# Attention key-value tails as full-row matmuls over zero-padded values, with a new instruction order

## The chip, the cores and the metric

The kernel runs on one core of a Trainium2 chip. The time is device microseconds of one execution of the whole kernel; the median of a few executions counts, and less is better. A profile is one further execution, recorded instruction by instruction.

## What is computed

Linear attention with cosine weights over 8 batches, 8 heads, 576 positions and a head dimension of 64, followed by a two-layer network with a squared ReLU on the 4608 x 512 result (weights 512 x 2048 and 2048 x 512):

```python
def phi(x, c, s):
    r = np.maximum(x, 0.0)
    return np.concatenate([r * c, r * s], axis=-1)
q_p = phi(q, cos_w, sin_w)
k_p = phi(k, cos_w, sin_w)
kv = np.einsum('bhsf,bhsd->bhfd', k_p, v)
z = np.sum(k_p, axis=2)
num = np.einsum('bhsf,bhfd->bhsd', q_p, kv)
den = np.einsum('bhsf,bhf->bhs', q_p, z)[..., None] + 1e-06
attn = num / den
...
h = x @ w_in
r = np.maximum(h, 0.0)
g = r * r
y = g @ w_out
```

## The kernel before

**Attention.** The 576 positions of a batch are four tiles of 128 positions (j = 0 to 3) and a tail of 64 (j = 4, in the code `J`). The tails of an even and an odd batch share tiles: the even batch's 64 positions lie in partitions 0 to 63, the odd batch's in 64 to 127 (`rows(b)`). Raw tails are loaded into `kt`, `vt` and `qt`, one load for each batch. The features of key tails go to `kpt`; from batch 2 on, one instruction with all 128 partitions makes them for both batches of a pair. The values are cast to bf16 by `att_v` into `vext` (four tiles, two buffers, by `b % 2`) and into `vextt` (the tail; two buffers, by `b // 2 % 2`, each holding a pair of batches). Column 64 of each head in these tiles is one, so that one product gives the sums and the normalizer together.

`att_kv` (matmuls at L400) multiplies key features by values: 8 heads x 4 tiles of 128x65 with 128 partitions contracted, then 8 tail matmuls with the batch's own 64 partitions. `att_kvz` copies the result to SBUF, `att_num` (L526) multiplies by query features, and `att_div` divides. Batch 0 has a path of its own (`first_ones`, `first_kv`; L414 and L431). Query features are transposed on TensorE for batches 0 and 1 (`att_qT_pe`, L499), by DMA later.

**The two layers.** The work is done per batch of 512 positions (m = 0 to 7), with the tails of all batches as a ninth block (m = 8). From block 2 on each product is made from seven half-size products instead of eight: L698 for the first layer, L887 for the second, both 128x256 matmuls. Between products with a shared accumulator ScalarE copies PSUM banks (`seed`: L1108 and L1190; others at L1125, L1200 and L1213) and applies the ReLU (L714); VectorE adds (L721, L1196), squares (L631), and forms sums of operands (L656, L680, L847, L866). Earlier blocks use plain products (L615, L748, L774, L788). L382 are filler matmuls on zeros, at the start and in the first stage.

**The order.** The program first records every step as an operation of a plan (`add`: engines, duration, reads, writes), and each reading or writing of a named resource orders it behind others. `ORDER` is a written-out list of all operations with an engine for each (`p` TensorE, `a` ScalarE, `v` VectorE, `g` GpSimd, `s` the DMA queue of SyncE). `Plan.run` records them in exactly this order, so each engine's queue, the SyncE queue included, has the order of the list. Many features, casts and squares can go to either ScalarE or VectorE; the list says which. `plan_v` and `plan_kv` add the operations for values and the key-value product. The loads of the main tiles are at L218, of tails at L257, DMA transposes at L490 and L558, stores at L813.

Of the kernel before, what the change touches and what calls it, by code (L numbers as in the profile page):

```python
# [15 lines left out]
FP = 512  # L16
# [9 lines left out]
117v 128a 122p 138a 145v 129p 143a 306v 140a 124p 83g 123a 146p 130a 84g 148p 125a 147v 131p 126a
149v 133p 85g 171v 168v 150p 166v 134a 142v 167a 151p 169v 132a 172v 152p 174v 170a 173v 135a 153p
86g 154p 87g 155p 156p 177v 88g 176a 178v 175a 181p 179v 180v 182p 183p 157p 250s 184a 89g 332v 185p
158p 253s 186v 159p 257s 258s 191p 189p 254s 187p 192v 160p 251s 190v 252s 195p 188v 161p 196v 255s
193p 162p 194a 334v 199p 197p 249s 163p 200v 164p 198v 256s 285v 201p 278v 165p 202a 286v 279a 209p  # L30
207v 210p 203a 218p 280v 211a 261v 206a 259v 215p 260v 281a 216p 264v 212p 219a 262v 282s 221p 217a
263v 284v 283a 227p 271v 266a 272v 287s 269v 225p 270a 268v 265a 273v 213p 267v 222a 274p 307v 421s
226a 275p 214a 276p 230p 309v 277a 420s 228a 234p 204v 231a 288p 223p 235a 299s 289v 244p 298s 224a
419s 290p 229a 232p 291v 236p 220v 292s 233a 293p 239p 245a 294v 237a 418s 241p 240a 416s 439v 238a
295p 441v 246p 445v 296v 310p 247a 311p 440v 438a 297s 301v 242a 312p 444v 308v 300a 417s 313p 243a
302s 248v 314p 443a 333v 344p 424a 446v 315p 427v 423a 447s 428v 422a 316p 340v 429v 425a 341v 345p
342v 360p 431v 346a 361p 426v 317p 347a 432v 442s 430v 362a 343v 348p 433v 363a 349p 350a 303p 364p
205s 351a 304v 365p 366a 573s 353p 352p 367a 355v 434p 354v 368p 458s 369p 358v 574s 356p 370v 435p
459s 371v 357a 436p 208s 372p 374v 437a 397p 572s 335v 373a 381p 569s 319v 398a 448p 396p 318a 571s
449v 380p 399a 321p 570s 382a 359v 400p 383a 568s 401p 402a 450p 384p 403a 451v 322p 386a 597a 405p  # L40
601v 452s 453p 599a 385p 407v 404p 454v 387a 323p 566s 594a 406v 388p 305s 375a 389p 390v 324p 391v
565s 392p 460a 410v 408p 376v 393a 455p 325p 394v 409a 456v 411a 326p 378v 457s 327p 395v 596a 328p
567s 577v 493p 329a 330v 509p 580a 412v 466p 461a 595v 468p 602v 600a 462s 575v 584a 469p 578v 603s
414v 585a 467p 489v 470a 576v 581v 510p 598s 471a 490v 494p 377v 511a 474p 495a 583v 491v 512a 475p
379v 589a 320s 337v 513p 496a 717s 514p 492v 515a 463p 413v 497p 516a 464v 498p 718s 586a 517p 331s
499a 518p 579v 472p 519v 500a 588a 415v 501p 587a 590p 582a 503v 713s 521p 520v 502p 714s 522a 591p
336v 716s 592p 523v 546p 504v 593a 505p 547a 339v 545p 506a 604p 338v 530p 548a 529p 605v 531a 473p
476a 507v 532a 606p 735v 549p 477a 607v 533p 551a 550p 535a 534p 737v 608s 552a 609p 741v 478p 736v
536a 610v 738a 715s 537p 524a 553p 539v 554p 538p 555v 611p 556v 480p 729a 612v 508a 557p 479p 540v
613s 742v 541p 558a 482v 481p 542a 739s 559v 743a 485p 543v 740v 544a 560v 486p 744s 657p 637v 641p  # L50
727v 487a 730v 642p 721a 638v 488s 658p 483v 643a 614p 640v 659a 484s 720v 615p 644a 871s 561v 660a
639v 868s 645p 724a 525v 661p 870s 725a 646p 723v 869s 722v 662p 663a 562v 616p 647a 864s 728v 664a
527v 617p 865s 648a 526v 719a 666p 563v 618a 649p 726a 665p 651v 650p 863s 619a 731p 668v 862s 653p
667v 732p 652v 654a 755s 733p 669p 671v 734a 756s 655v 677p 528v 670a 694p 867s 745p 693p 695a 746v
678p 696a 622p 679a 656v 747p 680a 697p 897a 620p 748v 894a 681p 891v 892a 749s 698p 672v 699a 750p
682p 700a 623p 866s 896v 683a 751v 465s 702p 684a 701p 898a 673v 685p 893a 686p 687v 621p 624a 703v
882a 752p 564v 689p 625a 705p 886a 753v 626p 899a 704v 706a 754s 628p 758a 884v 707v 627p 690a 688v
895s 877a 629p 691v 630v 692a 790p 875v 900s 633p 757v 631v 634p 872a 786v 708v 759s 791p 635a 807p
792a 787v 806p 709v 763p 793a 789v 885a 883v 794p 808a 788v 1010s 795p 675v 796a 764p 1011s 809a
881v 710v 880a 632s 765p 876v 797a 810p 878v 874a 879v 798p 812a 873v 799p 800v 811p 1013s 760p 711v  # L60
1012s 813a 802p 761v 766p 1014s 1015s 814p 801v 767a 887p 636s 816v 803a 888p 1053s 768a 804v 889p
1027v 1052s 815p 712v 890a 771p 805a 817v 826p 674v 762s 901p 843p 1025v 820v 827p 1026a 902v 818p
844a 769p 819a 676v 828a 772p 821v 829a 903p 770p 773a 904v 830p 774a 842p 1024v 905s 832a 1016v
906p 831p 822v 845a 775p 1021v 833a 1018v 1017a 846p 907v 847p 848a 776p 1019v 849a 1022v 908p 1032a
835p 909v 851p 1037a 834p 1033a 850p 853v 910s 1034a 777p 779v 1038a 852v 778p 1020a 836v 782p 1054a
780v 1023a 854p 837v 1035a 838p 934v 1028p 855a 856v 1036s 935v 955p 839a 823v 939p 956a 936v 938p
857v 940a 954p 1029p 941a 1030p 825v 957a 783p 1031a 840v 937v 1040a 958p 841v 942p 784a 1042p 960a
959p 1039v 944a 943p 858v 1041s 1055a 911p 1043v 945a 912p 961a 859v 785s 963p 860v 781s 947p 861v
946p 1056s 962p 965v 913p 948v 914p 949v 964v 950p 915a 1044p 968v 966p 951a 952v 975p 824v 916a
974p 967a 1045v 991p 976a 919p 953v 977a 1046s 990p 992a 1047p 917p 993a 1048v 969a 978p 994p 995p  # L70
979p 996a 970v 1049p 920p 997a 972v 980a 998p 1050v 921a 918p 981a 1000v 1051s 999p 922a 971v 982p
983p 984v 925p 985v 986p 1001v 1002p 987a 988v 923p 1004v 1003a 1083v 924p 1005a 1084v 1085v 1088p
927v 1104p 1087p 1086v 1089a 989v 930p 1090a 1105a 1057p 1006v 1091p 1092p 1007v 1093a 1103p 931p
1008v 1094a 1106a 1058v 926p 932a 1095p 1059s 928v 1107p 1108p 1097v 1109a 1096p 933s 1009v 1062p
1110a 929s 1098v 1112p 973v 1111p 1101v 1099p 1114v 1063p 1100a 1113v 1124p 1117v 1064a 1140p 1125a
1123p 1182v 1115p 1126a 1060p 1116a 1141a 1127p 1118v 1128p 1129a 1139p 1061p 1130a 1142a 1132p
1065a 1143p 1134v 1144p 1145a 1131p 1183v 1068p 1146a 1184v 1102a 1133v 1147p 1148p 1137v 1187p
1149v 1135p 1119v 1188a 1069p 1136a 1150v 1151p 1070a 1153v 1203p 1138v 1152a 1066p 1204a 1202p
1121v 1067p 1185v 1205a 1154v 1186p 1071a 1207p 1189a 1120v 1206p 1072p 1155v 1208a 1073p 1157v
1209a 1156v 1190p 1076v 1191p 1192a 1211p 1079p 1193a 1213v 1074p 1195p 1194p 1197v 1080p 1210p  # L80
1081a 1196v 1075p 1082s 1200v 1198p 1212v 1239p 1158v 1199a 1223p 1240a 1216v 1214p 1077v 1222p
1215a 1159p 1122v 1078s 1224a 1217v 1238p 1225a 1161p 1241a 1201v 1227p 1226p 1243p 1228a 1162p
1229a 1242p 1218v 1163a 1160p 1244a 1220v 1231p 1246a 1245v 1230p 1164a 1233v 1247p 1248p 1232v
1165p 1249v 1236v 1234p 1250v 1251p 1235a 1167p 1252v 1254a 1237v 1168p 1255v 1166p 1253v 1169a
1260p 1170a 1219v 1261p 1256v 1257v 1171p 1262a 1258v 1172p 1173p 1175v 1174p 1263p 1176v 1178p
1259v 1177s 1221v 1179p 1264p 1180a 1268p 1181s 1265a 1269p 1266g 1267g 1271p 1270a 1272p 1274p
1273a 1275p 1281p 1276a 1277a 1282p 1278v 1286p 1280g 1283v 1279g 1290p 1285s 1287a 1289g 1284s
1291a 1288g 1293a 1292s
"""


class Plan:

# [49 lines left out]
def kernel(  # L143
# [9 lines left out]
    nc = tc.nc  # L153
    P = nc.NUM_PARTITIONS
    B, H, S, D = q.shape
# [1363 lines left out]
```

## Time and profile before

| | us |
|---|---|
| runs | 272.72, 273.38, 273.41 |
| median | 273.38 |
| profiled execution, its own time | 272.29 |
| span in its profile | 270.5 |
| TensorE busy | 264.0 (98%) |
| VectorE busy | 217.1 (80%) |
| ScalarE busy | 199.3 (74%) |

PE is TensorE's matmul side and PEld its weight loads, DVE is VectorE, ACT ScalarE, POOL GpSimd, SP SyncE with its DMA queue. `L400` is line 400 of the kernel. A row of the timeline has the start, the length in us, engine, line, operation, output and inputs, the shapes, and the count of merged instructions; in square brackets stand the idle time of the engine before and what ended it. The chain is the work that ended last, followed back from the end. A matmul's record includes its way through the array, so the records of a dense stream overlap, and its pace is read from starts or from the chain's pieces.

### The profile page before, as it was taken

Reading aid. Unit: us, or ns where it says so; the run is one execution under the profiler, and the core shown is the slowest. Engines: PE = TensorE matmul, PEld = TensorE weight load, DVE = VectorE, ACT = ScalarE, POOL = GpSimd, SP = SyncE. Lnnn points to the kernel's source line nnn. Section 1 sums busy time; section 2 is a strip of 40 time slices with the busy share of each in tenths; the row PEclk is TensorE's granted clock in tenths of the full one; section 3 lists DMA queues with packets and bytes.
Section 4 is the critical chain, followed back from the end, with each engine's and each line's share of the span. In section 5 each row is a group of like instructions: output and inputs, shape, how many; then the busy total and the mean of one; then the engine's idle time right before and its main releaser. Section 6 shows DMA issues by size and latency. Waiting matters only on the chain.

```text
span 270.5 us, 6697 instructions
## 1 busy us (share of the span) xinstructions
PE 264.0 (98%) x2710; PEld 212.8 (79%) x2710; DVE 217.1 (80%) x455; ACT 199.3 (74%) x330; POOL 18.6 (7%) x33
## 2 busy tenths in 40 slices
PE   8999999999999999999999999999999999999993
PEld 3787555655587688998999889899988888888882
DVE  1774866898978999999999999999799679779401
ACT  3885971699969989899899978994966696373131
POOL 8345000000000000000000000000000000000013
PEclk9999999999999999999999999999999999999999
DMA  7999999799999999989999999639311300210134
GB/s 210 256 206 287 321 258 358 199 247 261 285 288 307 250 228 254 384 169 235 284 277 199 213 348 314 83 80 271 41 40 41 139 0 0 80 78 4 78 119 116
DMA packets 86142, 52.79 MB, mean 195 GB/s; under 512 B 56960, under 2 KB 82944, under 8 KB 86112
## 3 DMA queue, kind: packets, MB, share of 16 engines
q1 hardware_dynamic: 78624, 42.87, 61.3%
q0 software_dynamic: 7136, 9.37, 16.0%
q8 instruction: 21, 0.34, 0.5%
q10 hardware_dynamic: 352, 0.13, 0.2%
q14 instruction: 9, 0.07, 0.1%
HBM read 36.70 MB, written 9.44 MB: 171 GB/s over the span
## 4 chain that ended last, share of the span: by engine, by line
PE 90%; DMA 6%; DVE 0%; SPq 0%; ACT 0%; issue 0%; POOL 0%; POOLq 0%; DVEq 0%
PE bank L698 32%; PE bank L887 31%; DMA q<-in_q_dram 6%; PE bank L615 6%; PE bank L774 5%; PE bank L788 5%; PE abank L400 3%; PE abank L526 3%; PE bank L499 1%; PE bank L599 1%; PE bank L431 1%; PE abank L382 0%; DVE qp L358 0%; PE bank L563 0%; SPq L245 0%
## 5 line engine op out<-in xcount | busy, mean ns | idle before, releaser
L698 PE MATMUL bank<-xT,w1sb 128*128 128x256 bf16 x336 | 47.7, 273 | 0.0
L698 PEld LDWEIGHTS <-w1sb 128*128 128x128 bf16 x448 | 42.7, 98 | 6.3
L887 PEld LDWEIGHTS <-gT 128*128 128x128 bf16 x448 | 43.6, 98 | 5.1
L714 ACT ACTIVATE gT<-bank 128x512 bf16<-128x512 f32 x56 | 32.6, 598 | 15.2 <-PE bank L698 14.9
L887 PE MATMUL bank<-w2sb,gT 128*128 128x256 bf16 x336 | 41.9, 273 | 0.0
L721 DVE TENSOR_TENSOR gT<-bank,qpTp 128x512 bf16<-128x512 f32 x56 | 36.7, 685 | 5.7 <-PE bank L698 5.3
L887 PEld LDWEIGHTS <-gs 128*128 128x128 bf16 x336 | 32.7, 98 | 3.7
L698 PEld LDWEIGHTS <-w1t 128*128 128x128 bf16 x336 | 32.2, 98 | 4.1
L1108 ACT COPY bank<-bank 128x512 f32<-128x512 f32 x56 | 31.8, 581 | 3.1 <-PE bank L698 1.8
L698 PE MATMUL bank<-qpTp,w1t 128*128 128x256 bf16 x224 | 31.5, 273 | 0.0
L887 PE MATMUL bank<-w2t,gs 128*128 128x256 bf16 x224 | 28.0, 273 | 0.0
L629 ACT ACTIVATE gT<-gT 128x2048 bf16<-128x2048 bf16 (+1 forms) x15 | 27.8, 1855 | 0.3
L631 DVE TENSOR_TENSOR gT<-gT 128x2048 bf16<-128x2048 bf16 (+1 forms) x19 | 22.5, 1191 | 1.3 <-ACT gT L714 1.2
L541 DVE TENSOR_TENSOR x<-abank,rden 128x512 bf16<-128x512 f32 x30 | 20.7, 692 | 1.0
L615 PE MATMUL bank<-xT,w1sb 128*128 128x512 bf16 x84 | 19.9, 379 | 0.0
L821 POOL DMA_DIRECT2D out_dram<-ysb x4 | 2.4, 614 | 235.3 <-ACT ysb L1200 230.5
L1196 DVE TENSOR_TENSOR ysb<-bank,y 128x512 f32<-128x512 f32 x14 | 9.6, 688 | 10.7 <-ACT bank L1249 7.6
L1125 ACT COPY qpTp<-bank 128x512 f32<-128x512 f32 x28 | 16.2, 590 | 0.6 <-PE bank L698 0.6
L698 PE MATMUL bank<-xT,w1t 128*128 128x256 bf16 x112 | 16.3, 273 | 0.0
L698 PE MATMUL bank<-zeros,w1sb 128*128 128x256 bf16 x112 | 16.0, 273 | 0.0
L1200 ACT COPY ysb<-bank 128x512 f32<-128x512 f32 x13 | 7.6, 587 | 10.6 <-PE bank L887 10.5
L774 PE MATMUL bank<-w2sb,gT 128*128 128x512 bf16 x64 | 15.1, 379 | 0.0
(128 smaller groups left out, 432.8 us busy)
## 6 DMA issues: line engine op xcount, KB each, us to landing
out_dram<-ysb SPq DMA_DIRECT2D x16, 512.0 KB, 4.1
q<-in_q_dram SPq DMA_DIRECT2D x13, 512.0 KB, 6.9
v<-in_v_dram SPq DMA_DIRECT2D x12, 512.0 KB, 5.4
k<-in_k_dram SPq DMA_DIRECT2D x12, 512.0 KB, 6.5
w1sb<-in_moe_w_in_dram POOLq DMA_DIRECT2D x4, 512.0 KB, 9.7
w2sb<-in_moe_w_out_dram POOLq DMA_DIRECT2D x4, 512.0 KB, 15.2
k<-in_k_dram SPq DMA_DIRECT2D x1, 1024.0 KB, 5.6
q<-in_q_dram POOLq DMA_DIRECT2D x1, 1024.0 KB, 9.2
```

The lines of the kernel that those rows point to most:

```text
L541: nc.vector.tensor_tensor(out=x[:, :], in0=n4[:, :, :, 0:D].rearrange("p b (k l) d -> p b k l d", l=2), in1=rden[:, :] .rearrange("p b (k ...
L615: nc.tensor.matmul(out=out_, lhsT=w1sb[:, kb, hb * P : (hb + 1) * P], rhs=x_block(m, kb), start=(kb == 0), stop=(kb == KB - 1),)
L629: eng.activation(out=g, in_=g, func=ACTF.Square)
L631: eng.tensor_tensor(out=g, in0=g, in1=g, op=ALU.mult)
L698: nc.tensor.matmul(out=bank[to][:, s * W : (s + 1) * W], lhsT=lhs[:, kb, (2 * u + s) * P : (2 * u + s + 1) * P], rhs=rhs[:, kb, :], start= ...
L714: nc.scalar.activation(out=g_pair(m, i, j, u), in_=bank[to][:, :].rearrange("p (s c) -> p s c", s=2), func=ACTF.Relu,)
L721: nc.vector.tensor_tensor(out=g_pair(m, i, j, u), in0=bank[to][:, :].rearrange("p (s c) -> p s c", s=2), in1=in_five(u).rearrange("p (s c) ...
L774: nc.tensor.matmul(out=bank[FIRST_Y[tt]][:, :], lhsT=gT_of(0)[:, hb, tt * P : (tt + 1) * P], rhs=w2sb[:, hb, :], start=(hb == 0), stop=(hb ...
L788: nc.tensor.matmul(out=bank[LAST_Y[s_]][:, :], lhsT=gT_of(m)[:, hb, tt * P : (tt + 1) * P], rhs=w2sb[:, hb, :], start=(hb == 0), stop=(hb ...
L887: nc.tensor.matmul(out=bank[to][:, s * DM2 : (s + 1) * DM2], lhsT=lhs[:, hb, s * P : (s + 1) * P], rhs=rhs[:, hb, :], start=(fresh and hb ...
L1108: add("ACT", psum, lambda: nc.scalar.copy(out=bank[b][:, :], in_=bank[a][:, :]), r=[("bank", a)], w=[("bank", b)])
L1125: add("ACT", psum, lambda u=u, Y=Y: nc.scalar.copy(out=in_five(u), in_=bank[Y][:, :]), r=[("bank", Y)], w=five)
```

## The change

From batch 2 on, the tail values of an even batch go to one tile and those of an odd batch to another (`vextt` is now chosen by `b % 2`), each in the batch's own 64 partitions. The other 64 partitions of each tile are set to zero once, at the start. The tail matmuls of the key-value product then use all 128 partitions: the other batch's key features meet zeros. Batches 0 and 1 keep 64 partitions. The cast of a pair's tail values becomes two casts, one for each batch, with operations of their own in the plan. One more filler matmul is planned in the first stage (7 instead of 6). The list of operations is new; the queues of SyncE and GpSimd keep their order, those of TensorE, ScalarE and VectorE don't, and of the operations that may go to either engine 42 move from ScalarE to VectorE and 41 the other way.

```diff
         nc.vector.memset(vx[:, :, :, D:E1], 1.0)
-        nc.vector.memset(vxt[:, :, D:E1], 1.0)
+
+        nc.vector.memset(vxt[rows(1 - i), :, :], 0.0)
+        nc.vector.memset(vxt[rows(i), :, D:E1], 1.0)
...
-    def att_v(b, j, eng, ps=ALL):
+    def att_v(b, j, eng):
         copy = eng.copy if eng is nc.scalar else eng.tensor_copy
         if j < J:
             copy(out=vexts[b % 2][0][:, j, :, 0:D], in_=piece("v", b, j))
         else:
-            copy(out=vexts[b // 2 % 2][1][ps, :, 0:D], in_=piece("v", b, j)[ps])
+            copy(out=vexts[b % 2][1][rows(b), :, 0:D], in_=piece("v", b, j)[rows(b)])
...
     def att_kv(b, js):
-        vx, vxt = vexts[b % 2][0], vexts[b // 2 % 2][1]
+        vx, vxt = vexts[b % 2]
...
-                        lhsT, rhs = kp_of(b, j)[rows(b), h, :], vxt[rows(b), h, :]
+                        ps = ALL if b >= 2 else rows(b)
+                        lhsT, rhs = kp_of(b, j)[ps, h, :], vxt[ps, h, :]
...
     def plan_v(b, j, eng=None):
-        ps, gs = parts_of(b, j)
-        add_either(FP, "cast", lambda e: att_v(b, j, e, ps), in_keys("v", b, j),
-                   [("v", b % 2, j)] if j < J else [("vt", b // 2 % 2, g) for g in gs], eng)
+        _, gs = parts_of(b, j)
+        for c in (b,) if j < J else [b - b % 2 + g for g in gs]:
+            add_either(FP, "cast", lambda e, c=c: att_v(c, j, e), in_keys("v", c, j) if j < J else [("vt", c % 2)],
+                       [("v", b % 2, j)] if j < J else [("vtx", c % 2)], eng)
...
-                    ("kpt", b % 2, "c"), ("kpt", b % 2, "s"), ("vt", b // 2 % 2, b % 2)]
-            add("PE", 0.268 * len(js), lambda js=js: att_kv(b, js), r=r, w=[("T",)], due=due + n * step)
+                    ("kpt", g, x) for g in (range(2) if b >= 2 else (b % 2,)) for x in "cs"] + [("vtx", b % 2)]
+            add("PE", 0.268 * len(js) - 0.02 * (js == (J,)), lambda js=js: att_kv(b, js), r=r, w=[("T",)], due=due + n * step)
...
-    for i in range(6):
+    for i in range(7):
         add("PE", 0.216, lambda: warm(1), w=[("T",)], due=20.0, after=9.2)
```

The list `ORDER` itself, some 1,300 entries, is left out here.

More of the change, by code (lines that the diff above doesn't have):

```diff
@@ L26 @@
[L26 to L50, printed above, removed]
@@ L84 @@
[L84 to L88, printed above, removed]
+0p 14a 15v 13v 10a 9v 11v 16a 12v 17a 8v 19a 18v 1p 32p 24v 23a 20p 33p 34p 21v 35p 25p 22v 36a 2p
@@ new lines @@
+68p 42p 26a 37p 43v 27a 38p 28g 39p 58v 40p 50p 46p 59v 41a 47a 51v 3p 4p 69p 44p 60p 63a 52p 45v
+54p 61a 64a 55v 5p 6p 7p 48p 62v 92p 29g 94p 53v 49a 74p 65p 75v 56p 91p 66a 93p 95p 96p 57v 67a 76p
+30g 73p 98p 97p 77v 78p 100a 102p 99a 79v 71p 103p 109p 101v 31g 80p 70p 110p 111a 81v 104p 105p
+106a 119p 112a 82g 107a 114p 113v 120a 108v 121p 116a 128p 143v 141a 115p 83g 139v 138v 123p 140v
+117a 137v 122a 147p 118v 129a 145p 144v 124a 125p 148v 142a 84g 146v 130p 126a 85g 149p 127v 131a
+132p 150v 134p 86g 171a 308v 167a 151p 135a 174v 152p 168a 169v 175v 133a 153p 173v 170a 176v 87g
@@ new lines @@
+154p 172v 136a 155p 88g 156p 157p 89g 178v 177a 180v 182p 179v 181a 183p 184p 72p 158p 251s 185a 90g
+334v 186p 159p 254s 187v 160p 258s 259s 192p 188p 255s 193v 190p 161p 252s 191v 253s 196p 189v 194p
+162p 197v 195a 256s 163p 336v 198p 200p 250s 164p 199v 201v 165p 257s 286v 202p 282v 166p 203a 283v
+280a 210p 208v 211p 207a 219p 287v 281a 288v 212a 264v 216p 284s 267v 262a 217p 263v 222p 220a 266v
+274a 261v 213p 265v 204a 214p 285v 218a 228p 270v 289s 260a 271v 273v 226p 272a 268v 223a 309v 276p
@@ new lines @@
+269a 423s 277p 215a 335v 278p 227a 231p 221v 422s 279a 235p 232a 337v 290p 224p 236a 301s 291v 229a
+245p 300s 275a 205v 225a 421s 292p 237p 230a 293v 233p 294s 295p 240p 234a 296v 238a 420s 242p 446a
+440v 418s 445a 297p 442v 247p 246a 298v 241a 312p 243a 303v 299s 248a 313p 441v 244a 239v 314p 419s
+448a 310v 315p 249a 316p 447v 430a 427v 346p 426v 302a 317p 311v 425a 304s 449s 318p 443a 342v 431a
+343v 347p 424v 363p 345v 348a 362p 433v 444s 319p 344v 349a 432v 364a 434v 350p 428v 365a 351p 352a
@@ new lines @@
+305p 206s 366p 353a 306v 575s 367p 368a 354p 355p 435v 369a 356v 436p 429a 460s 370p 576s 358p 372v
+437p 461s 359a 357v 438p 209s 371p 439a 360v 374p 574s 373v 383p 375a 571s 450p 376v 399p 320a 321v
+573s 398p 384a 451v 382p 572s 400a 323p 401a 377v 570s 385a 324p 452p 402p 453v 386p 404a 387p 388a
+403p 361v 454s 455p 325p 405a 456v 389a 568s 406p 463a 407p 307s 408v 600a 390p 391p 409v 597a 410p
+392v 462a 567s 457p 326p 412v 603a 393v 411a 327p 378v 413a 396v 394p 586v 328p 458v 329p 395a 339v
@@ new lines @@
+459s 583a 330p 397v 605a 511p 569s 331a 332v 495p 579a 464s 468p 414v 582a 598v 470p 577a 380v 379v
+580a 471p 604v 602a 469p 491v 472a 585v 606s 599v 496p 492v 473a 512p 493v 497a 476p 338v 601s 513a
+415v 477p 514a 587v 498a 494v 515p 589a 322s 578v 516p 588a 417v 720s 499p 517a 500p 416v 501a 465p
+474p 518a 721s 466v 502a 333s 519p 581a 503p 521v 590a 520p 591a 504p 381v 716s 523p 584a 522v 717s
+593p 524a 505v 719s 594p 525v 595p 341v 548p 596a 507p 506v 549a 547p 340v 508a 607p 532p 550a 608v
@@ new lines @@
+531p 533a 475p 478a 740v 534a 609p 551p 479a 610v 535p 553a 552p 537a 536p 509v 611s 745v 554a 612p
+480p 538a 613v 510a 718s 555p 539p 743v 614p 557v 540p 541v 526a 556p 559p 542v 543p 615v 481p 560a
+730v 482p 741a 616s 558v 738a 483p 484v 544a 561v 487p 739a 545v 744v 546a 742s 562v 488p 660p 640v
+644p 746v 489a 645p 725v 747s 661p 724v 646a 617p 641v 485v 662a 647a 618p 642v 490s 726v 723a 486s
+527v 649p 663a 648p 874s 563v 733a 665p 871s 731v 650a 664p 565v 728a 619p 873s 643v 666a 872s 564v
@@ new lines @@
+620p 651a 722v 867s 729a 732v 652p 566v 667a 653p 621a 592v 734p 655v 727a 868s 668p 654v 669p 622a
+735p 866s 670v 736p 865s 528v 681p 737a 672p 671v 682a 656p 530v 758s 673a 748p 697p 658v 657a 759s
+696p 749v 698a 680p 870s 625p 699a 674v 683a 901v 750p 900v 897a 626p 529v 898a 751v 684p 685p 686a
+700p 675v 752s 701p 687a 753p 702a 623p 754v 889a 869s 703a 624p 467s 627a 659v 689p 885a 704p 628a
+691v 688p 902a 755p 706v 705p 887a 895v 631p 760a 756v 896a 629p 886a 883v 757s 630p 690v 903a 761a
@@ new lines @@
+694v 632p 899s 633v 884a 708p 707v 692p 634v 709a 636p 904s 693a 710v 789v 637p 695a 711v 793p 762s
+875v 810p 790v 809p 638a 888v 794p 878v 811a 766p 712v 795a 1014s 676v 767p 796a 1015s 791v 812a
+713v 798p 880a 797p 876v 635s 768p 792v 799a 882v 879v 813p 800a 877v 814p 881a 763p 815a 802p 1017s
+764v 801p 816a 1016s 769p 1018s 804v 817p 1019s 803v 770a 891p 819v 639s 771a 892p 677v 1057s 805p
+818p 715v 1056s 806a 893p 821p 820v 1028a 765s 830p 894a 807v 829p 1029v 890a 905p 823v 772p 822a
@@ new lines @@
+906v 831a 773p 832a 679v 808a 907p 678v 845p 833p 714v 846p 908v 834p 835a 774p 836a 824v 909s 847a
+775p 848a 1023v 910p 1021v 838p 776a 911v 850p 777a 849p 1042a 837p 1022v 778p 851a 840v 852a 839v
+912p 1027a 779p 1020v 913v 1038a 853p 1025a 854p 855v 914s 841p 1030a 1032p 1031v 1039a 782v 780p
+1037a 1044v 842a 1043v 781p 856v 1024a 785p 1026v 1041a 843v 1036a 938v 857p 859v 942p 939v 1040s
+858a 943p 825v 1033p 940v 944a 1034p 783v 958p 1045s 1035a 844v 959p 945a 786p 960a 941v 946p 860v
+961a 947p 948a 1046p 962p 787a 827v 963p 949a 788s 861v 915p 964a 784s 1058v 965a 916p 863v 1059a
@@ new lines @@
+1047v 966p 1060s 951p 968v 917p 953v 1048p 918p 1049v 967p 919a 970p 1050s 969v 950p 920a 1051p 971a
+972v 979p 952v 923p 1052v 980a 995p 954p 862v 996a 1053p 924p 955a 864v 826v 978p 925a 994p 828v
+981a 921p 1054v 997a 982p 999p 956v 1055s 984a 983p 957v 998p 985a 922p 1000a 987p 1001a 1061p 926a
+989v 1002p 973a 986p 1087v 1003p 1004v 927p 988v 1005v 928p 974v 990p 992v 1006p 1088v 991a 1108p
+1008v 1007a 1089v 1092p 1062v 1091p 1093a 1107p 1109a 929p 1009v 1063s 1110a 930p 1094a 931v 993a
+1095p 1090v 932v 1096p 1111p 975v 1112p 1097a 976v 934p 1113a 1010v 1098a 935p 1012v 1114a 1099p
@@ new lines @@
+1011v 936a 1116p 1101v 1100p 937s 1115p 1118v 933s 1103p 1013v 1066p 1104a 1117v 1067p 1102v 1105v
+1144p 1128p 1145a 1127p 1186v 1129a 1119p 1106v 1064p 1130a 1120a 1131p 977v 1132p 1121v 1133a 1143p
+1065p 1134a 1068a 1135p 1146a 1136p 1069a 1137v 1148p 1147p 1138v 1072p 1187v 1149a 1141v 1073p
+1188v 1150a 1151p 1074a 1152p 1153v 1191p 1139p 1154v 1192a 1155p 1157v 1140a 1070p 1156a 1142v
+1207p 1206p 1208a 1122v 1071p 1209a 1190p 1189v 1075a 1210p 1123v 1193a 1211p 1158v 1212a 1078p
+1213a 1194p 1124v 1195p 1125v 1196a 1076p 1159v 1197a 1077p 1161v 1198p 1080v 1215p 1214p 1217v
@@ new lines @@
+1199p 1083p 1201v 1084p 1243p 1216v 1085a 1227p 1079p 1200v 1086s 1244a 1228a 1202p 1126v 1218p
+1203a 1163p 1220v 1219a 1081v 1226p 1160v 1082s 1242p 1204v 1229a 1165p 1162v 1245a 1221v 1230p
+1231p 1232a 1247p 1205v 1246p 1233a 1164p 1248a 1166p 1250a 1249v 1234p 1167a 1251p 1236v 1252p
+1168a 1235p 1253v 1171p 1254v 1238p 1256v 1237v 1255p 1239a 1169p 1257v 1258a 1240v 1170p 1241v
+1172p 1259v 1264p 1260v 1173a 1261v 1265p 1174a 1262v 1177p 1222v 1266a 1178p 1223v 1175p 1180v
+1176p 1225v 1181s 1263v 1267p 1179v 1268p 1224v 1182p 1269a 1183p 1270g 1271g 1272p 1184a 1273p
@@ L89 @@
+1185s 1275p 1274a 1276p 1278p 1277a 1279p 1285p 1280a 1281a 1286p 1282v 1290p 1284g 1287v 1283g
+1294p 1289s 1291a 1293g 1288s 1295a 1292g 1297a 1296s
 """
```

38 lines of the change are left out of this document (removed).

## The prediction

> **What bounds the kernel now.** I read the page first (busy shares, slices, the chain by engine), then the busy time of each engine in stretches, then the chain in order of time, and last the single instructions around the step that the change edits.
>
> ```profile
> PE 264.0 (98%) x2710; PEld 212.8 (79%) x2710; DVE 217.1 (80%) x455; ACT 199.3 (74%) x330; POOL 18.6 (7%) x33
> ...
> PE   8999999999999999999999999999999999999993
> ...
> PE 90%; DMA 6%; DVE 0%; SPq 0%; ACT 0%; issue 0%; POOL 0%; POOLq 0%; DVEq 0%
> ```
>
> PE is busy 98% of the span and holds 90% of the chain; what is missing lies in the first and the last slice. DVE and ACT are not far behind on average, so the stretches matter:
>
> ```profile
> 28.00:66.00 38.00, 38.00 (x341) 22.06 (x340) 29.87 (x67) 27.11 (x43) 0.00 (x0) 1.00 1.06 273
> ...
> 96.00:123.00 27.00, 27.00 (x311) 24.15 (x310) 26.21 (x58) 25.38 (x42) 0.00 (x0) 1.00 1.01 256
> 123.00:148.00 25.00, 25.00 (x281) 22.55 (x280) 23.79 (x51) 23.46 (x43) 0.00 (x0) 1.00 1.11 254
> ...
> 230.00:250.00 20.00, 20.00 (x186) 17.94 (x184) 16.26 (x26) 9.43 (x17) 0.00 (x0) 1.00 0.14 54
> ```
>
> Columns after the length are PE, PEld, DVE and ACT busy, POOL, the granted clock (1.00 throughout). From 28 us on PE has no idle time that this view can show, while DVE and ACT, at 26.21 and 25.38 of 27 us in one stretch, have 0.8 and 1.6 us to spare: the kernel is bound by the PE stream, with two engines close behind in the middle. A matmul's record is longer than its place in the stream, so small holes don't show as idle. They show in the chain, as pieces that last longer than their count:
>
> ```profile
> 17.20 9.16 DMA q<-in_q_dram
> 26.39 0.90 DVE qp L358 x2
> 27.33 0.62 PE bank L499 x8
> ...
> 78.70 0.48 PE abank L400 x16
> 79.18 1.31 PE bank L698 x12
> 80.49 0.83 PE abank L400 x24
> 81.33 1.42 PE bank L698 x12
> ...
> 245.76 19.23 PE bank L887 x176
> ```
>
> L400 is the key-value product. Sixteen of its matmuls take 0.48 us and are followed by twelve of L698 in 1.31, which is 12 x 0.109. The group that ends in the eight tail matmuls takes 0.83 for 24, and the same twelve behind it take 1.42. The stretch of 176 at the end has 19.23 / 176 = 0.109 each, no hole at all.
>
> **The switch that is removed.** Around that group, one matmul at a time (start, length, form):
>
> ```profile
> 80.33 0.65 PE L400 MATMUL abank<-vext,kp 128*128 128x65 bf16 x16
> ...
> 80.78 0.19 PE L400 MATMUL abank<-vext,kp 128*128 128x65 bf16 x1
> 80.91 0.23 PE L400 MATMUL abank<-vextt,kpt 64*128 64x65 bf16 x2
> ...
> 81.14 0.19 PE L400 MATMUL abank<-vextt,kpt 64*128 64x65 bf16 x1
> 81.26 0.28 PE L698 MATMUL bank<-zeros,w1sb 128*128 128x256 bf16 x1
> ```
>
> The sixteen 128-row matmuls start from 80.33 to 80.78: fifteen steps of 0.030. The first 64-row one starts 0.13 behind the last of them, 0.10 more than a step; the last 64-row one is followed 0.12 later, 0.09 more than a step. The eight tails themselves start from 80.91 to 81.14, seven steps of 0.033, no faster than full rows. So one tail group costs two holes, 0.19 us. That L400 is followed by L698 without a hole at 79.18 says that the change of rows makes them, not the change of line. The change gives tail matmuls of batches 2 to 7 all 128 rows, the form of the others, and leaves batch 1 and the first batch as they are: six groups, 6 x 0.19 = **-1.14 us**, all in the stream that sets the end. The seventh group of the 56 tail matmuls, batch 1, keeps its holes. Bounds: nothing (the hole belongs to something else), and -6 x 0.22 = -1.32 from the chain's pieces (0.83 - 0.48 - 8 x 0.03 = 0.11, 1.42 - 1.31 = 0.11).
>
> The Trainium skill, "TensorEngine Tiling (Array Packing)", Tiling Modes, says that changing the tiling mode drains TensorE and changing only the tile doesn't; "TensorE: Matmul & The Clock Gate", Part 2, puts the drain at some 128 cycles, of 2.4 GHz when warm. An estimate by these pages is 0.053 us a switch, 12 x 0.053 = -0.64 us; the rows have almost twice that, and I keep the rows.
>
> **What is added.** The casts of tail values (L378) become two of 64 rows for a pair of batches, where one of 128 rows did both.
>
> ```profile
> 38.54 0.42 DVE L376 CAST vext<-v 128x512 bf16<-128x512 f32 x1
> 38.99 0.43 DVE L378 CAST vextt<-vt 64x512 bf16<-64x512 f32 x1
> 39.45 0.69 DVE L847 TENSOR_TENSOR w2t<-w2sb 128x1024 bf16<-128x1024 bf16 x1
> ...
> 55.92 0.43 DVE L378 CAST vextt<-vt 128x512 bf16<-128x512 f32 x1
> 56.26 0.48 DVE L358 TENSOR_SCALAR kpt<-kt,cos_col 128x512 bf16<-128x512 f32 x1
> ...
> 102.27 0.64 ACT L378 CAST vextt<-vt 128x512 bf16<-128x512 f32 x1
> 102.79 0.61 ACT L1108 COPY bank<-bank 128x512 f32<-128x512 f32 x1
> ```
>
> A cast costs by its columns, not by its rows: 0.43 with 64 and with 128 rows. On DVE it occupies 0.34 (55.92 to 56.26); the one that starts at row 64 occupies 0.46 and waits about 0.1 in front (38.54 to 38.99). On ACT it occupies 0.52. Before: two on DVE, two on ACT. After, in the new list: one on DVE (batch 5), six on ACT, so ACT has 4 x 0.52 = 2.1 us more and DVE 0.3 less, over 220 us. Of the features, value casts and squares, 42 go from ACT to DVE and 41 the other way, which about evens out. None of it lies on the path as long as ACT's spare time covers it (1.6 us in the 96 to 123 stretch, where one or two of the casts fall): 0. Two memsets of 64 x 520 are new at the start of DVE; both engines then wait for the keys until 6.4 us: 0.
>
> The cast of batch 5 now stands alone and late, and SP's load of batch 7's tail values must wait for it, since both use the lower half of one tile. Behind it in SP's queue stand the value, query and key loads and the transposes for batch 5.
>
> ```profile
> 130.56 3.19 SPq L257 DMA_DIRECT2D vt<-in_v_dram  x2
> ...
> 138.79 2.92 SPq L558 DMA_TRANSPOSE xT<-x  x1
> ...
> 142.38 1.19 SPq L558 DMA_TRANSPOSE xT<-xt  x1
> ...
> 145.45 1.23 SPq L558 DMA_TRANSPOSE xT<-x  x1
> ```
>
> Between 143.57 and 145.45 SP idles 1.9 us, so a wait up to that is taken in; the cast stands in the list about 1.8 us of PE work ahead of batch 5's tail group, close to where the load stands. I take 0; past 1.9 us each further microsecond would count.
>
> **The front.** There is one more filler matmul (L382, 0.22 us of PE). PE is caught before and after it: at 9.79 it waits 0.3 for query features, and at 27.33 for the features of batch 1's queries, whose load lands at 26.36.
>
> ```profile
> 27.33 0.62 PE L499 MATMUL bank<-ident,qp 128*128 128x128 bf16 x8 [0.33 <-DVE qp L358]
> ...
> 11.74 0.21 PE abank L382
> ```
>
> The new list puts one more unit (four matmuls of 0.216) ahead of these transposes, and its first transposes need the fourth of DVE's features, not the second. Two features take 0.90 and one 0.48, so they come 0.42 apart; the fourth ends at 26.39 + 3 x 0.42 + 0.48 = 28.13, and the transposes, 0.04 behind it as before, start at 28.17. At the same point of the stream the kernel before is at 27.33 + 0.86 = 28.19. PE itself would be there at 28.19 - 0.33 + 0.22 = 28.08, so the filler is swallowed, if the load lands as before. **0**, between -0.33 (the wait goes) and +0.22 (the filler counts).
>
> **The reordered stream.** The list is new on PE, ACT and DVE, while SP and POOL keep theirs, and the last twelve products are in the same order. What the new order costs can't be seen in this trace; how little it may slip can:
>
> ```profile
> 100.32 0.57 ACT L1190 COPY bank<-bank 128x512 f32<-128x512 f32 x1 [0.34 <-PE bank L887]
> ...
> 100.94 0.60 PE L887 MATMUL bank<-w2sb,gT 128*128 128x256 bf16 x4
> ```
>
> The copy ends at 100.89 and its product starts at 100.94 without having waited: 0.05 us to spare. I compared how much PE work the two lists put between a product and the next that needs its copy: 0.87 us at this place in both, and 1.1 to 1.3 us at some thirty others in both. No margin is cut, so I take **0** new waits; the bounds are 0 and some 3 us (the second rival).
>
> **Sum.** -1.14 and nothing else. The profiled execution took 272.29 us (span 270.5, 1.8 around it); after, 271.15. The median of the runs is 273.38, 1.09 above it, so in medians **272.2 us**.
>
> **Rivals.**
> 1. The waits come back in part (chance 0.20). For: ACT gains 2.1 us of casts, its handoffs have 0.05 us and upward to spare, and every tail group that goes faster brings PE 0.19 earlier to them. If two of the four additional casts stand ahead of a copy with nothing to spare, 2 x 0.52 = 1.0 returns: 273.3, within 0.3% of before. Against: the equal margins of the two lists.
> 2. ACT becomes the bound between 96 and 148 us and the kernel gets slower (0.13). There DVE has 50.0 of 52 us and ACT 48.8. If the six casts on ACT all show on the path, 6 x 0.52 = 3.1 us: 273.38 - 1.14 + 3.1 = 275.3. It decides for slower once 2.0 of the 3.1 aren't covered. Against: the moves between the engines relieve ACT about as often as they load it, and ACT has 3.2 us free there.
> 3. Full rows cost more than they save (0.04). Today's tails then run at half the work. The skill's tiling page, Overview, promises up to twice the speed for a contraction of at most 64, which speaks against giving the halves up. As a mechanism here: two halves would run at once, 0.12 us for eight, and full rows would add 6 x 0.12 = 0.7: 272.9. The rows speak against it: 0.033 a step with 64 rows, 0.030 with 128.
> 4. The change doesn't do what it says (0.04): the holes belong to the tile of keys, not to its rows, and stay. Then 273.4.
>
> **How the numbers follow.** Forecast 0.59, rivals as above. The runs before lie up to 0.66 below and 0.03 above their median, and I allow 0.35 each way for scatter. The likeliest case alone: 273.38 - 1.32 - 0.33 = 271.7 to 273.38 - 1.14 + 0.22 = 272.5, with the scatter 271.4 to 272.8. Rivals 1, 3 and 4 end at 272.9 to 273.4, with the scatter at 273.8; two thirds of the second rival's price give 274.3. Range 271.4 to 274.3: what is left out is the dearer half of rival 2 and the far ends. What a measurement of this kernel can tell from no change is about 0.3%, 0.82 us: faster is below 272.56, slower above 274.20. The forecast gives 0.52 of its 0.59 to faster, and rival 1 0.04; rival 2 and a few slips of the first go to slower.
>
> **What would show it.** Right: tail matmuls in the form 128*128 128x65, no hole at their ends; the chain's groups of 24 at 0.72 instead of 0.83; PE in unbroken steps from 28 us; transposes of L499 near 28.2. Wrong: PE idle before L887 or L698 released by ACT copies between 96 and 148 us (rivals 1 and 2), holes of 0.1 that stay (4), tails slower than 0.033 a step (3), a wait of SP at L257 near 132 us that moves the transposes.

## The result, and the profile after

| | before | after |
|---|---|---|
| median, us | 272.95 (272.43 to 274.04, 22 runs) | 274.28 (273.16 to 275.52, 22 runs) |
| ratio | | 1.0048, 95% interval 1.0035 to 1.0062 |
| profiled execution (span) | 272.29 (270.5) | 275.19 (273.4) |

The changed kernel is slower by 1.3 us, where 1.2 us less was forecast (272.2, with a range of 271.4 to 274.3). The two profiled executions lie further apart, by 2.9 us: that of before is 0.7 under its median, that of after 0.9 over it. The profiles say where time goes; the medians say how much.

First the page after: busy times, then the chain by engine.

```profile
PE 264.3 (97%) x2711; PEld 212.3 (78%) x2711; DVE 220.6 (81%) x457; ACT 196.0 (72%) x333; POOL 18.6 (7%) x33
...
PE 77%; DMA 10%; DVE 9%; issue 1%; SPq 1%; ACT 0%; POOL 0%; POOLq 0%; DVEq 0%
```

PE held 90% of the chain and DMA 6%; now PE has 77, DMA 10 and DVE 9. ScalarE, which the second rival expected to become the bound, is not in it. What PE waits for (us in all, times, the longest):

```profile
PE abank L529 <- DMA qpT<-qp: 1.2, 1, 1.2
PE abank L384 <- DVE zeros L272: 1.2, 1, 1.2
PE bank L701 <- DVE qpTp L683: 0.8, 1, 0.8
PE abank L529 <- DVE x L544: 0.6, 1, 0.6
PE bank L701 <- DMA xT<-x: 0.5, 1, 0.5
PE bank L502 <- DVE qp L360: 0.2, 1, 0.2
```

The second is the wait at the very start, as before. The others on PE's timeline, the tail group first:

```profile
80.09 0.65 PE L403 MATMUL abank<-vext,kp 128*128 128x65 bf16 x16
80.58 0.40 PE L403 MATMUL abank<-vextt,kpt 128*128 128x65 bf16 x8
80.82 0.60 PE L701 MATMUL bank<-xT,w1t 128*128 128x256 bf16 x4
...
94.61 1.24 PE L791 MATMUL bank<-w2sb,gT 128*128 128x512 bf16 x5
96.35 0.39 PE L701 MATMUL bank<-xT,w1sb 128*128 128x256 bf16 x2 [0.50 <-DMA xT<-x]
...
99.85 1.04 PE L890 MATMUL bank<-w2sb,gT 128*128 128x256 bf16 x8
101.68 0.49 PE L701 MATMUL bank<-qpTp,w1t 128*128 128x256 bf16 x3 [0.79 <-DVE qpTp L683]
...
140.54 0.60 PE L701 MATMUL bank<-qpTp,w1t 128*128 128x256 bf16 x4
141.74 0.40 PE L529 MATMUL abank<-kvz,qpT 128*128 128x65 bf16 x8 [0.60 <-DVE x L544]
...
182.35 0.60 PE L701 MATMUL bank<-qpTp,w1t 128*128 128x256 bf16 x4
184.20 0.42 PE L529 MATMUL abank<-kvz,qpT 128*128 128x65 bf16 x8 [1.25 <-DMA qpT<-qp]
```

The tail group has the form 128*128 and no hole: eight matmuls from 80.58, the next line 0.24 later, 0.030 each. The first step of the forecast is there. But four waits are new. A record overlaps the next, so a wait is longer than its bracket: the four matmuls of 182.35 fill 4 x 0.109 = 0.44, the next was due at 182.79 and starts at 184.20, 1.41 late. In the same way 0.66, 0.95 and 0.76 are lost at 95, 100 and 141 us. With the 0.34 of the front (transposes of batch 1's queries at 28.53, where the kernel before stood at 28.19) the pair of profiles closes: -1.14 + 3.78 + 0.34 = +3.0, against 273.4 - 270.5 = 2.9.

In the chain in order of time three of the longest pieces are transfers, and each stands ahead of one of the waits:

```profile
95.59 5.51 DMA xT<-x
...
131.46 7.69 DMA q<-in_q_dram
...
179.06 5.09 DMA qpT<-qp
```

The busy times by stretch show in what these transfers run. The last two columns are the DMA engines' share and GB/s:

```profile
96.00:123.00 27.00, 25.86 (x299) 23.09 (x300) 23.87 (x55) 24.63 (x42) 0.00 (x0) 1.00 1.11 271
123.00:148.00 25.00, 24.40 (x276) 21.94 (x275) 23.57 (x51) 23.23 (x41) 0.00 (x0) 1.00 1.02 260
...
175.00:203.00 28.00, 26.75 (x309) 23.76 (x308) 24.75 (x50) 20.08 (x34) 0.00 (x0) 1.00 0.51 114
```

PE lacks 1.14, 0.60 and 1.25 us in these three. In the first two the DMA share was above 1 before as well (the prediction's rows show 1.01 and 1.11), in the third it is 0.51. Full DMA engines could thus have a part, in the waits at 95, 100 and 141 us above all; an experiment below tries it.

SyncE's queue has the same order in both kernels, but its entries leave later. In the kernel before:

```profile
119.47 1.24 SPq L558 DMA_TRANSPOSE xT<-x  x1
120.81 4.92 SPq L490 DMA_TRANSPOSE qpT<-qp  x2
...
129.17 0.69 SPq L218 DMA_DIRECT2D q<-in_q_dram  x1
...
133.85 2.37 SPq L218 DMA_DIRECT2D v<-in_v_dram  x2
...
176.51 7.24 SPq L490 DMA_TRANSPOSE qpT<-qp  x2
```

and after:

```profile
120.91 1.23 SPq L561 DMA_TRANSPOSE xT<-x  x1
123.49 4.52 SPq L493 DMA_TRANSPOSE qpT<-qp  x2
...
131.46 0.71 SPq L218 DMA_DIRECT2D q<-in_q_dram  x1
132.22 0.61 SPq L257 DMA_DIRECT2D kt<-in_k_dram  x1
132.87 3.25 SPq L257 DMA_DIRECT2D vt<-in_v_dram  x2
136.22 2.28 SPq L218 DMA_DIRECT2D v<-in_v_dram  x2
...
179.06 4.91 SPq L493 DMA_TRANSPOSE qpT<-qp  x2
```

Batch 5's transposes leave 2.7 us later, the load of batch 6's queries behind them 2.3, batch 7's first transpose 2.55. Not all of this comes from the queue. The transpose of `x` ahead of batch 5's leaves 1.44 later already, about as late as PE itself is by then (0.34 + 0.66 + 0.95 - 3 x 0.19 = 1.38). From it to batch 5's are 1.34 us before and 2.58 after: in these 1.24 us the queue stands for a feature, and all behind it waits too. Batch 7's transpose belongs to the product that starts at 184.20 after, 182.79 without its wait, and in the kernel before here:

```profile
181.27 0.41 PE L526 MATMUL abank<-kvz,qpT 128*128 128x65 bf16 x8
```

The product's place is 1.52 later, so of the 2.55 only 1.03 count against it. ScalarE, just before this transpose:

```profile
177.09 0.71 ACT L356 ACTIVATE kp<-k,cos_col 128x512 bf16<-128x512 f32 x1
177.71 1.32 ACT L356 ACTIVATE qp<-q,cos_col 128x512 bf16<-128x512 f32 x2
```

The second of these two query features ends at 179.03, and the transpose leaves at 179.06: the new list puts the feature that the transpose needs last, behind a key feature and one for batch 7's other transpose.

### The profile page after: what moved, and what is told of

Same layout as the page of the kernel before. It is cut to its first block, busy times and chain, and to the rows that moved or that the text cites. A ratio compares the mean times of both kernels' runs of the same rounds, so it can differ in the third digit from the quotient of the medians.

```text
span 273.4 us, 6701 instructions
## 1 busy us (share of the span) xinstructions
PE 264.3 (97%) x2711; PEld 212.3 (78%) x2711; DVE 220.6 (81%) x457; ACT 196.0 (72%) x333; POOL 18.6 (7%) x33
## 4 chain that ended last, share of the span: by engine, by line
PE 77%; DMA 10%; DVE 9%; issue 1%; SPq 1%; ACT 0%; POOL 0%; POOLq 0%; DVEq 0%
PE bank L890 26%; PE bank L701 26%; DMA q<-in_q_dram 6%; PE bank L618 5%; PE bank L777 5%; PE bank L791 3%; PE abank L384 3%; PE abank L529 3%; PE abank L403 2%; DMA xT<-x 2%; DMA qpT<-qp 2%; DVE qp L360 2%; DVE gT L724 1%; PE bank L502 1%; PE bank L602 1%
## 5 line engine op out<-in xcount | busy, mean ns | idle before, releaser
L890 PE MATMUL bank<-w2sb,gT 128*128 128x256 bf16 x336 | 41.1, 273 | 0.0
L634 DVE TENSOR_TENSOR gT<-gT 128x2048 bf16<-128x2048 bf16 x22 | 26.6, 1217 | 0.4 <-ACT gT L717 0.2
L632 ACT ACTIVATE gT<-gT 128x2048 bf16<-128x2048 bf16 (+1 forms) x12 | 21.2, 1779 | 0.1
```

Source lines behind the costliest of these rows:

```text
L632: eng.activation(out=g, in_=g, func=ACTF.Square)
L634: eng.tensor_tensor(out=g, in0=g, in1=g, op=ALU.mult)
L890: nc.tensor.matmul(out=bank[to][:, s * DM2 : (s + 1) * DM2], lhsT=lhs[:, hb, s * P : (s + 1) * P], rhs=rhs[:, hb, :], start=(fresh and hb ...
```

## The experiments

Two theories stood at the start. A: the tail change is worth its 1.1 us, and the new order loses more in a few places. B: the DMA engines are full, so PE waits back whatever it gains, in any order. Ratios below are to the kernel before, timed beside each run. Where two runs are compared by their ratios, the difference is uncertain by 0.2 to 0.3%, 0.6 to 0.7 us. A profile is one execution; those of the runs with moves and lighter loads lie up to 1.7 us above their medians, so the waits read from them are not typical sizes. Line numbers shift by one or two between kernels, so rows are best read by their tiles.

**The tail change in the old order.** Before's list, with each pair's two casts where the one cast stood:

```
-    for i in range(7):
+    for i in range(6):
 ORDER: as before; 273v -> 273v 274v, 589a -> 590a 591a, 886a -> 888a 889a (renumbered)
```

> The tail change alone: full-row tails over zeros and the two casts per pair, in the order of the kernel before (six fillers, each pair's two casts next to each other where the one cast stood). Theory A, the new order lost the time: 12 switches of 0.095 us go and nothing comes back, so 1.1 us less than before, ratio to before about 0.996, and no wait on PE over 0.3 us between 28 and 200 us. Theory B, the DMA engines bound the stretch from 28 to 175 us, so that whatever PE gains there it waits for at the next transpose: ratio 0.999 to 1.001, with new waits of about 1 us in all for transposes. Theory C, full rows or the extra casts cost by themselves: ratio over 1.001.

272.60 us, ratio 0.9991 (0.9974 to 1.0008): B's number, with A's 0.996 outside the interval. The waits are not B's, though. Laid beside the profile of before, matmul by matmul, the twelve holes are gone, 0.08 to 0.11 each, 1.2 us in all; 0.36 comes back at 104.9 us, for a copy and not for a transpose. PE and then ScalarE, there:

```profile
104.46 0.60 PE L700 MATMUL bank<-qpTp,w1t 128*128 128x256 bf16 x4
105.25 0.60 PE L700 MATMUL bank<-xT,w1sb 128*128 128x256 bf16 x4 [0.19 <-ACT bank L1111]
```

```profile
102.23 1.26 ACT L379 CAST vextt<-vt 64x512 bf16<-64x512 f32 x2
...
104.63 0.57 ACT L1111 COPY bank<-bank 128x512 f32<-128x512 f32 x1
```

The second cast of 102.23 pushes the steps behind it on, the copy at 104.63 (103.95 before) with them, and PE waits for that copy. This is the first rival's mechanism (a cast ahead of a copy with nothing to spare), though not in the list it was forecast for. Another 0.17 comes back at 150.3 behind a transpose, and the rest of the difference between the two profiles lies in the start (last section).

**The casts apart.**

```
 ORDER: 591a (batch 5) behind 523a, just ahead of batch 4's copy 595a
        889a (batch 7) just ahead of 769a
```

> The tail change in the order of the kernel before, but the second cast of two pairs moved away from the first: that of batch 5 from 102.8 us to the idle 0.57 us of ScalarE ahead of batch 4's copy of the product (109 us), that of batch 7 from 144.8 us to the idle 1.16 us near 158 us. In the run without this PE waited 0.36 us at 104.9 for a ScalarE copy that stood behind the cast, and 0.17 us at 150.3 for a sum behind a transpose. Theory A: the first wait goes, about 0.35 us less than with the casts together, 0.5 to 0.9 us less than before. Theory B (DMA bound): the 0.35 us come back at a transpose, within 0.15 us of the run with the casts together.

272.14 us, ratio 0.9968 (0.9954 to 0.9982): faster than the kernel before and the changed one, and A's number. Against the casts together it is 0.23%, 0.6 us, no more than the uncertainty; the profile shows 0.36 of it. ScalarE now has the cast in the gap:

```profile
109.00 0.62 ACT L379 CAST vextt<-vt 64x512 bf16<-64x512 f32 x1
109.65 0.59 ACT L479 CAST kvz<-abank 128x520 bf16<-128x520 f32 x1
```

and the product of 105.25 starts at 105.08 without a wait. B, in its strict form, falls: in this order some 0.9 us of the gain stays.

**Only the rows undone, in that order.**

```
-                        ps = ALL if b >= 2 else rows(b)
+                        ps = rows(b)
```

> The order of the kernel before with the casts spread and the zeros, but tail matmuls with 64 rows: the full rows alone undone. If the 12 holes of 0.10 us are worth their sum in this order: 1.1 to 1.2 us above the run with full rows, that is 0.2 to 0.4 us above the kernel before. If part of the gain goes to waits for landings: 0.5 to 0.9 us above it, equal to the kernel before.

273.32 us, ratio 1.0016 (0.9999 to 1.0033). Against the full rows that is 1.0016 - 0.9968 = 0.0048, or 1.3 us with 0.6 either way; the forecast had 1.14. Casts and zeros alone thus cost some 0.4 us, if anything.

**The same edit in the new order.** The changed kernel with `ps = rows(b)`.

> The changed kernel with its new order and its zeros, but the tail matmuls with 64 rows again, so that the 12 switches are back. Theory A (order): the switches cost 0.19 us for each of six batches, but the waits at 95, 100, 141 and 183 us take in part of what lies ahead of them: 0.3 to 1.1 us above the changed kernel. Theory B (DMA): all of it is taken in, 0 to 0.2 us above the changed kernel. Theory C (full rows cost by themselves): below the changed kernel.

274.47 us, ratio 1.0053 (1.0030 to 1.0076), against the changed kernel's 1.0048: 0.1 us, with 0.7 either way. The holes are back in its profile, 0.10 each, and the waits are shorter by more: 0.65 at 95, 0.64 at 100, 0.44 at 141 and 0.46 at 183 us. In the new order the full rows are worth little or nothing, as B expected. That PE only comes earlier to the same landings fits the waits, but isn't shown by them alone, as those at 95 and 100 come and go (below). The order decides how much of the gain counts.

**The price of a switch.** Before's kernel with the tails alternating with the fourth tile, 16 changes of rows in a group instead of 2:

```
-        for n, js in enumerate(((0, 1), (2, 3), (J,))):
+        for n, js in enumerate(((0, 1), (2,), (3, J)) if b >= 2 else ((0, 1), (2, 3), (J,))):
...
-                for half in range(2):
+                for half, j in [(half, j) for half in range(2) for j in jj]:
```

> The kernel before with the price of a switch made large: in batches 2 to 7 the tail matmuls alternate with those of the fourth tile, so that 16 changes between 64 and 128 rows stand where 2 stood, 84 more in all. If a change of rows costs 0.095 us as the holes say: 84 x 0.095 = 8.0 us more than before (ratio 1.029), steps of about 0.125 us between the alternating matmuls. If the holes belong to the change of tile or line, or are a fixed cost of the group: 0 to 1 us more. The Trainium skill, TensorE: Matmul & The Clock Gate, Part 2, gives 128 cycles for the drain, by which an estimate is 84 x 0.053 = 4.5 us more.

281.48 us, ratio 1.0309 (1.0283 to 1.0336): 8.7 us for 84 switches, 0.104 each.

```profile
82.62 0.20 PE L400 MATMUL abank<-vextt,kpt 64*128 64x65 bf16 x1
82.76 0.20 PE L400 MATMUL abank<-vext,kp 128*128 128x65 bf16 x1
82.89 0.20 PE L400 MATMUL abank<-vextt,kpt 64*128 64x65 bf16 x1
83.03 0.20 PE L400 MATMUL abank<-vext,kp 128*128 128x65 bf16 x1
```

Steps of 0.135 where 0.030 is the pace. Both matmuls are of one line and alternate between two tiles; the tile changes in the full-row group too (80.58 above) and costs nothing there. Two holes of 0.09 and 0.10 also stand around each of the four groups of L526 with the form 128*64, where the columns change instead of the rows (from 76.40 on in the profile of before); the change leaves all eight. The 128 cycles of the Trainium skill ("TensorE: Matmul & The Clock Gate", Part 2), an estimate of 0.053 us, are half of what this run shows.

**Moves in the new order.** Three groups, all together and each alone:

```
 ORDER: group 95:  302a (batch 0's tail feature) behind 445a; 458v (batch 3's last division) ahead of 393v
        group 141: 901v 900v (batch 6's query features) behind 751v (batch 5's second division)
        group 183: 1036a (batch 7's last feature for its first transpose) behind 1037a
```

> The changed kernel with steps of the new order moved: the cosine feature of batch 0's query tail and no other of its kind some 5 us earlier on ScalarE, batch 3's last division ahead of a sum on VectorE, batch 5's second division ahead of two query features of batch 6 on VectorE, and the last feature that batch 7's first transpose needs 1.7 us earlier on ScalarE. Theory A (four single places of the new order): the waits at 141 and 183 us go, 0.76 + 1.41 = 2.2 us less than the changed kernel, up to 3.8 if those at 95 and 100 go too. Theory B (the DMA engines bound the stretch, as the copy with 64-row tails suggests, which took no longer than the changed kernel): the waits come back at other transposes, within 0.5 us of the changed kernel.

> One of the three groups of moves alone, in the changed kernel: batch 0's query-tail feature earlier on ScalarE and batch 3's last division ahead of a sum on VectorE, for the waits at 95 and 100 us (1.6 us together in the profile). Theory A (each wait is a place of its own and the gains add): the three groups moved alone are worth some 0.4 to 0.5 us each, 1.4 in all as moved together. Theory B (PE catches up with the next late landing or step, so a wait removed is taken over by the next): this one gives 0 to 0.3 us, since the waits at 141 and 183 us grow.

> Batch 5's second division ahead of two query features of batch 6 alone, for the wait at 141 us (0.76 us in the profile). Theory A: 0.4 to 0.8 us less than the changed kernel. Theory B: 0 to 0.3 us, the wait at 183 us grows, or a cast that waits for its load near 144 us holds the next copy.

> Batch 7's last query feature for its first transpose 1.7 us earlier alone, for the wait at 183 us (1.41 us in the profile). Behind it no wait follows that could take it over: by both theories 1.0 to 1.4 us less than the changed kernel; by theory B this one carries nearly all of what the three groups together gave (1.4 us), by theory A a third to a half of it.

| moved | us | ratio |
|---|---|---|
| none (the changed kernel) | 274.28 | 1.0048 (1.0035 to 1.0062) |
| group 95 | 274.81 | 1.0060 (1.0038 to 1.0083) |
| group 141 | 274.13 | 1.0044 (1.0025 to 1.0063) |
| group 183 | 273.13 | 0.9994 (0.9975 to 1.0013) |
| all three | 272.85 | 0.9992 (0.9971 to 1.0012) |

The gains don't add: group 183 has all of it, 0.54% or 1.5 us by the ratios, 1.15 by the medians. With group 95 moved its two waits are gone, and in that profile those behind grow: that at 141 from 0.76 to 1.52, with new ones of 0.42 at 145 and 0.77 at 152. The waits at 95 and 100 are also gone in group 141's profile, where nothing near them was moved, so they belong to some executions only; why is open. The wait at 183 stands in every profile of the new order without its move, with 0.95 to 1.6 us, and in none with it:

```profile
182.82 0.60 PE L700 MATMUL bank<-qpTp,w1t 128*128 128x256 bf16 x4
183.26 0.41 PE L528 MATMUL abank<-kvz,qpT 128*128 128x65 bf16 x8
```

Four steps of 0.109 lie between these two: no wait. With full rows and without the move the transpose always leaves 3.73 us ahead of its product's place (4.76 in the kernel before) and takes 4.9 to 5.3 us; with the move it leaves 5.43 ahead and takes 3.7 to 3.8. The second transpose follows 1.7 us behind in all of them, so it does not explain the longer landing, whose cause stays open. Behind this place PE waits in none of these profiles, and nothing takes the gain over. Ahead of it something does. ScalarE and VectorE, with all three groups moved:

```profile
144.11 0.62 ACT L377 CAST vext<-v 128x512 bf16<-128x512 f32 x1 [1.16 <-DMA v<-in_v_dram]
```

```profile
152.42 0.42 DVE L682 TENSOR_TENSOR qpTp<-xT 128x512 bf16<-128x512 bf16 x1 [2.05 <-DMA xT<-x]
```

PE is 2 us earlier at 141 here, and gives 1.23 back at 145, for a copy behind that cast, and 1.08 at 152, for that sum, in an execution 1.7 us above the run's median.

**Less to load.** The changed kernel with half of each value load left out for batches 3 to 7:

```
-        hs = slice(half * HH, (half + 1) * HH)
+        hs = slice(half * HH, half * HH + (HH // 2 if nm == "v" and b >= 3 else HH))
```

> The changed kernel with half of the value loads of batches 3 to 7 left out (two heads of four in each load; the rest of the tile keeps values of an earlier batch), 10 x 256 KB less in the DMA queue between 60 and 160 us, and nothing else changed. Theory B (transposes land late because the DMA engines are full): the waits at 95, 100 and 141 us, of 0.66, 0.95 and 0.76 us, go, 1.5 to 2.5 us less than the changed kernel; the one at 183 us, behind a late feature, stays in part. Theory A (features and divisions that stand late in the new order): the waits stay, within 0.5 us of the changed kernel.

273.64 us, ratio 1.0020 (1.0005 to 1.0034), 0.28% or 0.8 us below the changed kernel, with 0.6 either way: more than A and less than B expected. Its waits at 95 and 100 are gone, which proves little, as they come and go; those at 141 and 183 are 1.31 and 1.58 long. The loads can make a part of the loss; the move of group 183 alone gave more, 0.54%.

**The queue itself.** Group 183, and batch 5's query features ahead of a square:

```
 ORDER: 1036a behind 1037a; 741a 738a 739a ahead of 526a; 744v 746v ahead of 484v
```

> The changed kernel with batch 7's feature moved up as before, and batch 5's query features too: three on ScalarE ahead of a square of 1.9 us, two on VectorE ahead of a sum and two more steps. In the changed kernel SyncE's queue waits for these features until 123.5 and 125.3 us (116.3 and 122.1 in the kernel before, whose queue has the same order), and all the loads and transposes behind them leave 2.3 us later. Theory Q (the queue stands for late features, and its delay lands at PE near 141 and 152 us): the loads behind leave 1.3 to 2.5 us earlier, PE passes the product at 152 us about 1 us earlier, 0.4 to 1.0 us less than with batch 7's feature alone, ratio to before 0.996 to 0.998. Theory B (the DMA engines are full, so an earlier issue lands no earlier): within 0.3 us of the run with batch 7's feature alone, ratio 0.999 to 1.000.

> All moves together in the changed kernel: those of batch 5's and batch 7's query features, batch 0's tail feature, batch 3's last division and batch 5's second division. Theory Q: as with the two first alone or up to 0.4 us less, ratio to before 0.995 to 0.998. Theory B: ratio 0.999 to 1.000, as the moves without batch 5's features gave 0.9992. Like the tail change in the order of before (0.9968) only if every wait of the new order is gone.

273.09 us, ratio 0.9981 (0.9962 to 1.0001); with the groups 95 and 141 too 272.74, ratio 0.9986 (0.9958 to 1.0015). Both lie between what Q and B expected. SyncE's queue with the features moved (first kernel):

```profile
119.73 1.23 SPq L560 DMA_TRANSPOSE xT<-x  x1
121.06 5.13 SPq L492 DMA_TRANSPOSE qpT<-qp  x2
```

Batch 5's transposes follow the one ahead after 1.33 us here, 1.34 with all moves and 1.34 in the kernel before; in every profile of the new order without this move it is 2.57 to 2.59. So 1.24 us of SyncE's delay stood for these features, and they are gone. The rest of the step from 123.49 to 121.06 lies further up, in waits at 95 and 100 that this execution doesn't have. What PE gains by it isn't shown: the product at 152 passes at 151.81, with all moves at 151.10, and between 151.5 and 153.0 in the profiles without this move. In time it is 0.13%, 0.35 us, less than group 183 alone, inside both intervals. Even with all moves the new order stays 0.18%, 0.5 us, above the old one with the casts apart, inside the uncertainty too.

## Why the prediction was wrong

- **The switch, -1.14: right in mechanism and size.** Holes of 0.10 gone where they were forecast; 0.104 by the run with 84 more; 1.3 us by the pair in the old order that differs in rows alone. Rivals 3 and 4 fall with it. But that all of it lies in the stream that sets the end holds for the old list; in the new one the same pair differs by 0.1 us.
- **The casts, 0: right for this list.** None of the new waits stands behind a tail cast. In the old list two adjacent casts cost 0.36 in one profile, by the first rival's mechanism.
- **SP's wait for batch 5's cast, 0: right.** The pair of tail loads leaves 2.3 us later than before, as late as the queue ahead of it, and the value loads behind the pair 2.4 later (136.22, 133.85 before): the wait is taken in.
- **The front, 0: +0.34 in this profile.** The query load landed 0.29 later (26.65, not 26.36). The kernel with 64-row tails in the new order, the same up to there, has 28.87.
- **The reordered stream, 0: the step that failed.** It measured +3.8 in the profile and, from the medians, 1.33 + 1.14 = 2.5; against the tail change in the old order with the casts apart it is 1.0048 - 0.9968 = 0.0080, 2.2 us. The working compared, in the two lists, the PE work between a product and the next that needs its copy. That margin was indeed not cut: no wait in the changed kernel's profile has that form. What was cut are paths through transfers. At 141 us it is a load, two query features and a division behind them on VectorE. At 183 us, where a move brings the time back, it has five links: feature, place in SyncE's queue, transpose, landing, product. Before, batch 7's transpose landed at 180.25 for the product at 181.27, 1.0 us to spare. In the new list the feature let it go 1.03 later against the product's place, and the transpose took 5.1 instead of 3.7: 1.03 + 1.36 - 1.02 = 1.4, the wait. The first term is the list's; why the transpose took longer stays open, and so do the waits at 95 and 100. The order of every queue was on view before the run; the sentence "SP and POOL keep theirs" was taken to mean that the transfers keep their times.
- **The second rival, slower: right side, other engine.** ScalarE did less than before (196.0 us against 199.3) and appears in no wait of PE in the changed kernel's profile. That 274.28 lies just inside the stated range is luck: the upper end was two thirds of this rival's price, for six casts on ScalarE.

## What to carry to other kernels

When a list is reordered, check each transfer's issue, not only the compute handoffs: for every DMA whose source is computed, when its last input is ready in the new list, what stands behind it in the same queue, and how much its landing had to spare. Behind a first wait everything is late, so compare a transfer's issue with the place of its product and not with the clock. Where waits follow each other in series, removing an early one can merely move the wait on; here the last one carried the gain, so it is a good one to begin with. A local gain is tested best in the old order, with one thing changed: here the same full rows were worth 1.3 us in one list and 0.1 in the other.

## What was not expected of the hardware

The same 25 filler matmuls at the start took 6.48 us in the profile of before and 7.47 in that of the old order with full rows:

```profile
2.45 6.48 PE L382 MATMUL abank<-zeros 128*128 128x512 bf16 x25
```

```profile
2.45 7.47 PE L383 MATMUL abank<-zeros 128*128 128x512 bf16 x25
```

Their pace goes from 0.43 to 0.216 us each at a point that differs between executions by several matmuls. Of that second 0.37 is still there at 27.7 us. It may be a part of the scatter of about 1 us that these kernels show; no run separates it.
